# Attention and a residual MLP on one core: turning q and k in parts, other places for the weight sums, an earlier weight fetch and plain stores at the end

## The chip, the cores and the metric

The kernel runs on one core of a Trainium2 chip. The core has TensorE (PE, with its weight loads PEld), VectorE (DVE), ScalarE (ACT), GpSimd (POOL) and SyncE (SP), and 16 DMA engines that all of its queues share. The metric is the device time in microseconds of one execution; three runs of the kernel before gave 800.32, 802.85 and 801.59 us, a median of 801.59.

## The reference

Eight batches of 384 tokens. Grouped attention (16 query heads, 4 key heads, 64 wide) gives x of 384 x 1024 for each batch; then a token-mixing step and a two-layer MLP follow, each with a residual scaled by `lam`:

```python
scores = scale * np.matmul(q, k.transpose(0, 1, 3, 2))
attn = softmax(scores)
x = np.matmul(attn, v)                       # heads side by side: 384 x 1024
a1 = alpha1 * x + beta1
u = x + lam * np.einsum('ts,bsd->btd', w_tok, a1)
a2 = alpha2 * u + beta2
out = u + lam * (np.maximum(a2 @ w_ch1, 0.0) @ w_ch2)
```

`w_ch1` is 1024 x 4096, `w_ch2` 4096 x 1024. Inputs and output are float32.

## The kernel before

**Stages.** The attention of the first batch runs alone (`side(0)`). Then `main(0)` and `main(1)` compute the MLP of the first two batches, each in two phases: phase 0 is the first layer (32 row tiles of the hidden layer, bank `h`, L492), phase 1 the second (bank `ch`, L521). After that the six remaining batches go in three pairs, `pair(0)` to `pair(2)`; a pair does both of its layers with seven block products instead of eight, on sums and differences of blocks. Phase 0 of a pair is the first layer (banks X, Y, Z, L635), phase 1 the second (three banks C, one for each 128 tokens `ms`, L675), which runs through seven products `o` in the order 1, 2, 6, 5, 3, 7, 4 (`PLACE2`), each in two halves `h` of eight hidden tiles.

**Units and the plan.** Both generators `yield` after some matmuls; a yield is a unit. The order is written out by hand: `put(stage, phase, unit, work)` hangs work on a unit, and after that unit the work is emitted into the engines' queues, which run strictly in order. So the attention of the coming batches (`side(b)`) is strewn between the MLP's matmuls: `scores` (L272) and the exp on ACT (L281), `av` (L311, then on VectorE the chain L316, L319, L324, L326), `tok_flip` (L336, then L343, the spill of u to the output by SP at L236, L347, and the turn L359 by SP). In phase 1 of a pair a unit is four 512-wide matmuls; the side of the pair's first coming batch starts at unit 0, that of the second at unit 38.

**Turns.** q and k arrive by POOL's casting loads in `q_raw` and `k` and are turned to `qT` and `kT` by SP's transposing DMAs (`flip_q`, L168; `flip_k`, L164). There is one `qT` and one `kT`, so a turn waits for the scores that read them last. For a pair's second batch the five turns stood at units 33 to 37 of phase 1.

**Sums.** `sums_a(j)` (L534 to L537, four steps) forms the left operands from the turned tiles of both batches, so it waits for the turns L359. `sum_w1` (L571, L576) forms the sums of a group's two w1 chunks, `sum_w2` (L564) those of w2, which SP stores to DRAM (`w2s`, L551) and fetches back (L583) as 28 blocks for each pair.

**The ring.** w1 chunks and w2 blocks share six slots. When TensorE is done with a slot, `free` takes the next entry of `queue`: a casting load of a w1 chunk by POOL (L177) or a fetch of a w2 block by SP. Before, a next pair's first two chunks stood two entries ahead of the end of a pair's 28 fetches.

**Evictions and stores.** A product's result is read out of C by VectorE (L690, L695, L697), scaled by `lam` one unit or more later (`flush`, L606), and added into the output in DRAM by POOL's accumulating DMA (`store`, L477). In `main`, hidden tiles leave their bank by ACT (L500) or VectorE (L502), and the second layer's result by VectorE (L525).

Of the kernel before, what the change touches and what calls it, by code (L numbers as in the profile page):

```python
# [12 lines left out]
def kernel(  # L13
# [82 lines left out]
    def piece():  # L96
        i = turn[0] % 6
        turn[0] += 1
        return pad[:, i * 1024:(i + 1) * 1024]
# [60 lines left out]
        for h in range(0, Hq, G):  # L160
            nc.gpsimd.dma_start(out=qrs[b][:, h:h + G], in_=q[b, h:h + G].rearrange("h (p st) d -> p h st d", st=NST))

    def flip_k(b):
        nc.sync.dma_start_transpose(out=kT.rearrange("p h i s -> p (h i) s"),  # L164
                                    in_=k2s[b].rearrange("p h a st d -> p (h a st d)"))

    def flip_q(b, i=0, n=NP):
        nc.sync.dma_start_transpose(out=qT[:, i:i + n].rearrange("p a j s -> p (a j) s"),  # L168
# [312 lines left out]
    def main(b):  # L481
        a2T = a2Ts[b]
        n = S + 1 if b == 0 else S

        seq = order1[::-1 if b % 2 else 1]
        for i, c in enumerate(seq):
            for j in range(CW):
                nt = c * CW + j
                begun = b == 0 and nt in early
                ps = early[nt] if begun else bank([P, 512], "mm", "h")  # L490
                for dt in range(0 if begun else NDT):
                    nc.tensor.matmul(out=ps[:, :n], lhsT=w1[:, w1_slots[c], dt, j * P:(j + 1) * P],  # L492
                                     rhs=a2T[:, dt, :n], start=(dt == 0), stop=(dt == NDT - 1))
                    if dt == 3:
                        yield 0
                c1 = bias1[:, nt:nt + 1]
                if b == 0:
                    evac("DVE" if nt % 2 else "ACT")(out=c1, in_=ps[:, S:n])
                if nt % 2 == 0 or b:
                    nc.scalar.activation(out=hT[:, nt, :], in_=ps[:, :S], func=RELU, bias=c1)  # L500
                else:
                    nc.vector.tensor_scalar(out=hT[:, nt, :], in0=ps[:, :S], scalar1=c1,  # L502
                                            scalar2=0.0, op0=ADD, op1=mybir.AluOpType.max)
                yield 0
            if i + RING < NCH:
                w1_free.append(w1_slots.pop(c))
                load_w1(seq[i + RING])

            if b == 0 and i == NCH - RING:
                for dw, r, h in [(0, 1, 1)] + [(0, r, h) for r in (2, 3) for h in range(2)] + [  # L510
                        (1, r, h) for r in range(4) for h in range(2)]:
                    load_w2(dw, r, h)
                load_next(2)
        nts = [c * CW + j for c in seq for j in range(CW)]
        units = [(dw, ms) for dw in range(NDW) for ms in range(NST)]
        for k, (dw, ms) in enumerate(units):
            cs = slice(dw * 512, (dw + 1) * 512)
# [7 lines left out]
            nc.vector.tensor_tensor(out=o, in0=ps, in1=lam_t[:, cs], op=MUL)  # L525
# [59 lines left out]
    def free(slot):  # L585
        w1_free.append(slot)
        if queue:
# [1 line left out]
            f(*a)  # L589

    queue = [m for i in range(NB) for m in [(load_w1, c) for c in order1[2 if i else RING:]]
             + [(fetch, i, n) for n in range(SLOTS - 2)] + [(load_w1, c) for c in order1[:2] if i + 1 < NB]
             + [(fetch, i, n) for n in range(SLOTS - 2, SLOTS)]]

    IDENT = mybir.ActivationFunctionType.Identity
    SEQ1 = ((1, 0), (1, 1), (7, 0), (6, 0), (6, 1), (7, 1), (5, 0), (5, 1), (2, 0), (3, 0), (3, 1), (2, 1), (4, 0), (4, 1))
# [3 lines left out]
    def pair(i):  # L600
        b0 = NPL + 2 * i
        acc = pairs["acc"]

        def scaled(o, b, ms, dw, t):
            if o != 2:
# [61 lines left out]
        for k, o in enumerate(PLACE2):  # L667
            for h in range(2):
                for ms in range(NST):
                    if o == 4 and h and ms == NST - 1 and not last:  # L670
                        for n in (5, 7, 6, 4):
                            sum_w1(0, n)
                    for t in range(8 * h, 8 * h + 8):
                        slot = w2_slots[i, 4 * k + t // 4]
                        nc.tensor.matmul(out=X[ms], lhsT=hid[:, t, LEFT2[o], ms * P:(ms + 1) * P],  # L675
                                         rhs=ring[:, slot, t % 4 * 512:(t % 4 + 1) * 512],
                                         start=(o in (1, 6, 7) and t == 0), stop=(t == NH - 1), skip_group_check=True)
                        if t % 4 == 3 and ms == NST - 1:
                            free(slot)
                        if t % 8 == 3:  # L680
                            flush(1)
                            yield 1
                    if h == 1:
                        if o in (1, 6, 5):
                            q = ((1, 6, 5).index(o) * NST + ms) * 512
                            snap[o, ms] = snaps[:, q:q + 512]
                            if o == 1:
                                nc.scalar.copy(out=snap[o, ms], in_=X[ms])
                            else:
                                tt(out=snap[o, ms], in0=X[ms], in1=snap[1, ms], op=ADD)  # L690
                        else:
                            bb, dw = where[o]
                            t = spare(ms).bitcast(f32)
                            if o == 2:
                                tt(out=t, in0=X[ms], in1=lam_t[:, :512], op=MUL)  # L695
                            else:
                                tt(out=t, in0=X[ms], in1=snap[{3: 1, 7: 5, 4: 6}[o], ms], op=ADD)  # L697
                            later.append((scaled, o, b0 + bb, ms, dw, t))
                            if last and o == 4:
                                flush()  # L700
# [12 lines left out]
    with tc.manual_schedule(engines=order):  # L713
# [131 lines left out]
        def put(ps, phase, at, *m):  # L845
            plan.setdefault((ps, phase, at), []).append(m)
# [12 lines left out]
        put_all(0, 1, at)  # L859
        put_flips(0, 1, 2, (34, 36, 37, 42, 43))  # L860

        put(1, 0, 1, load_next, 3)
        put_all(1, 0, side(2)[1], lambda u: int(1.5 * u))
        put_flips(1, 0, 3, (53, 55, 57, 59, 61))
        put_all(1, 1, side(3)[1])
        for j, u in enumerate((33, 39, 43, 46)):
            put(1, 1, u, sums_a, j)
        for r in range(8):
            for i, o in enumerate((5, 6, 7, 4)):
                where = (1, 0, 30 + 16 * r + 4 * i) if r < 2 else (1, 1, 18 * (r - 2) + 4 * i) if r < 4 else (2, 0, 24 * (r - 4) + 1 + 6 * i)  # L870
# [61 lines left out]
```

## Time and profile before

| | before |
|---|---|
| runs, us | 800.32, 801.59, 802.85 |
| profiled execution, us | 794.35 |
| its span, first to last instruction, us | 792.5 |
| mean granted TensorE clock | 0.978 |
| TensorE busy, us | 745.1 |
| VectorE, ACT, POOL busy, us | 500.4, 327.3, 165.9 |
| from TensorE's last matmul to the end of the span, us | 8.1 |

TensorE and VectorE by stage (busy us of the length):

| stage | from to, us | TensorE | VectorE |
|---|---|---|---|
| `main(1)` phase 0 | 134 to 194 | 54.9 of 60 | 28.4 |
| `main(1)` phase 1 | 194 to 250 | 54.7 of 56 | 35.9 |
| `pair(0)` phase 0 | 250 to 332 | 77.5 of 82 | 65.7 |
| `pair(0)` phase 1 | 332 to 440 | 101.0 of 108 | 73.0 |
| `pair(1)` phase 0 | 440 to 524 | 77.0 of 84 | 59.2 |
| `pair(1)` phase 1 | 524 to 633 | 103.0 of 109 | 73.0 |
| `pair(2)` phase 0 | 633 to 712 | 74.5 of 79 | 58.6 |
| `pair(2)` phase 1 | 712 to 785 | 72.0 of 73 | 26.8 |

In the lines of a timeline the first number is the start in microseconds from the span's start, the second the duration; then come engine, source line, operation, the tiles (out<-in), the shape, and the count. Brackets hold the idle time of that engine just before, and what ended it. "SPq" is the DMA-issuing queue of SP; its duration is that of issuing, not of the transfer. In a list of waits the numbers are the total, how often, and the longest.

### The profile page before, as it was taken

What the parts mean: (1) busy time and instruction counts of PE and PEld (TensorE: products, weight loads), DVE (VectorE), ACT (ScalarE), POOL (GpSimd) and SP (SyncE); (2) the same over time, 40 slices, a digit from 0 to 9 for tenths busy, and PEclk for the clock granted to TensorE, in tenths of its full rate; (3) what the DMA queues carried; (4) which work ended last, traced back from release to release, by engine and by line L of the source; (5) the groups of instructions that cost most, each with busy time, mean ns of one, the idle gap of its engine ahead of it and who ended that gap; (6) DMA issues with size and microseconds to landing.
All of it is one profiled execution on the core that took longest, in us unless ns stands there. A gap on an engine that the chain in (4) does not pass through costs nothing.

```text
span 792.5 us, 14330 instructions
## 1 busy us (share of the span) xinstructions
PE 745.1 (94%) x5646; PEld 417.4 (53%) x5707; DVE 500.4 (63%) x975; ACT 327.3 (41%) x471; POOL 165.9 (21%) x214
## 2 busy tenths in 40 slices
PE   8999999998998999999997789999899889999995
PEld 5765555655554555555454356655445446654442
DVE  7663554454667788569576667738747677763333
ACT  7623332563340566643331266663233146660000
POOL 9434211410002310301022431121002221100012
PEclk9999999999998999999999899999999999999998
DMA  9999998999765999979889998997979999835786
GB/s 190 196 199 203 212 202 172 180 227 228 191 169 123 214 221 234 269 207 224 239 195 191 140 190 111 165 230 202 232 207 200 197 145 130 116 141 180 242 225 108
DMA packets 221536, 151.50 MB, mean 191 GB/s; under 512 B 92692, under 2 KB 200836, under 8 KB 221468
## 3 DMA queue, kind: packets, MB, share of 16 engines
q0 software_dynamic: 120736, 65.38, 63.4%
q1 hardware_dynamic: 100188, 84.80, 38.9%
q8 instruction: 44, 0.72, 0.4%
q10 hardware_dynamic: 544, 0.39, 0.2%
q14 instruction: 24, 0.20, 0.1%
HBM read 154.05 MB, written 38.27 MB: 243 GB/s over the span
## 4 chain that ended last, share of the span: by engine, by line
PE 68%; DMA 11%; issue 10%; DVE 7%; POOL 2%; ACT 1%; POOLq 0%; SPq 0%; DVEq 0%; ACTq 0%
PE C L675 15%; PE X L635 15%; PE ch L521 9%; PE Y L635 8%; DMA ops<-a 6%; PE h L492 6%; DMA w<-in_moe_w_ch_dram 4%; PE sc L272 4%; PE Z L635 4%; PE sc L336 2%; PE one L311 2%; PE sc L311 1%; POOL out_dram L477 1%; POOL w L177 1%; DMA qT<-q_raw 1%
## 5 line engine op out<-in xcount | busy, mean ns | idle before, releaser
L675 PE MATMUL C<-w,arena 128*128 128x512 bf16 x965 | 232.1, 383 | 2.4 <-issue 0.2
L281 ACT ACTIVATE es<-sc 128x1024 bf16<-128x1024 f32 x126 | 121.8, 1022 | 178.1 <-PE sc L272 171.8
L675 PEld LDWEIGHTS <-arena 128*128 128x128 bf16 x1008 | 92.8, 98 | 105.2 <-issue 11.1
L640 ACT ACTIVATE hT<-X,bias 128x384 f32<-128x384 f32 x144 | 83.7, 582 | 122.2 <-PE X L635 117.6
L635 PEld LDWEIGHTS <-w 128*128 128x128 bf16 x768 | 76.0, 99 | 70.9 <-issue 21.4
L477 POOL DMA_DIRECT2D out_dram<-hT x36 | 31.7, 881 | 283.0 <-DVE hT L606 179.8
L177 POOL DMA_DIRECT2D w<-in_moe_w_ch_dram x68 | 61.2, 906 | 141.7 <-PE X L635 63.2
L492 PE MATMUL h<-ops,w 128*128 128x384 bf16 (+1 forms) x480 | 84.4, 328 | 5.1 <-DMA w<-in_moe_w_ch_dram 3.6
L521 PE MATMUL ch<-arena,hT 128*128 128x512 bf16 x366 | 86.9, 379 | 0.9 <-issue 0.3
L635 PE MATMUL X<-ops,w 128*128 128x384 bf16 x384 | 72.7, 333 | 12.3 <-DVE hT L697 8.4
L635 PEld LDWEIGHTS <-pad 128*128 128x128 bf16 x576 | 57.5, 100 | 39.5 <-issue 3.7
L635 PE MATMUL X<-ops,pad 128*128 128x384 bf16 x384 | 73.3, 336 | 0.0
L492 PEld LDWEIGHTS <-w 128*128 128x128 bf16 x480 | 45.4, 98 | 35.5 <-DMA w<-in_moe_w_ch_dram 4.4
L343 DVE TENSOR_TENSOR xr<-sc,xr 128x384 f32<-128x384 f32 x56 | 31.1, 554 | 39.3 <-PE sc L336 39.3
L521 PEld LDWEIGHTS <-hT 128*128 128x128 bf16 x384 | 34.9, 98 | 37.7 <-issue 2.5
L336 PEld LDWEIGHTS <-wtokT 128*128 128x128 bf16 x576 | 37.7, 99 | 22.2 <-DVE a L326 12.7
L272 PE MATMUL sc<-qT,kT 64*128 64x384 bf16 (+2 forms) x576 | 44.7, 274 | 4.6 <-DMA qT<-q_raw 3.4
L311 PEld LDWEIGHTS <-es 128*128 128x128 bf16 x1008 | 39.4, 99 | 13.0 <-issue 1.2
L336 PE MATMUL sc<-a,wtokT 128*128 128x128 bf16 x504 | 38.3, 222 | 7.7 <-DVE a L326 7.6
L635 PE MATMUL Z<-ops,w 128*128 128x384 bf16 x192 | 39.0, 326 | 4.1 <-DVE arena L644 4.1
L635 PE MATMUL Y<-ops,w 128*128 128x384 bf16 x192 | 41.2, 339 | 0.3 <-DVE w L571 0.3
L642 DVE TENSOR_TENSOR arena<-Y,hT 128x384 bf16<-128x384 f32 x48 | 26.6, 557 | 23.1 <-ACT hT L640 20.9
(127 smaller groups left out, 835.8 us busy)
## 6 DMA issues: line engine op xcount, KB each, us to landing
w<-w2s SPq DMA_DIRECT2D x84, 512.0 KB, 5.0
w<-in_moe_w_ch_dram POOLq DMA_DIRECT2D x68, 512.0 KB, 9.3
out_dram<-xr SPq DMA_DIRECT2D x56, 192.0 KB, 4.7
out_dram<-hT POOLq DMA_DIRECT2D x36, 256.0 KB, 5.4
arena<-in_moe_w_ch_dram POOLq DMA_DIRECT2D x16, 512.0 KB, 19.1
w2s<-arena SPq DMA_DIRECT2D x28, 256.0 KB, 5.7
q_raw<-in_q_dram POOLq DMA_DIRECT2D x28, 192.0 KB, 8.9
w2s<-pad SPq DMA_DIRECT2D x16, 256.0 KB, 11.0
```

The source lines that it names most:

```text
L177: nc.gpsimd.dma_start(out=w1[:, w1_slots[c]], in_=w1src[:, :, c * CW * P:(c + 1) * CW * P])
L272: nc.tensor.matmul(out=sc[:, hh, k % 4:k % 4 + n], lhsT=kT[r, 2 * p // G, BLK[hh][sk], :], rhs=qT[r, p, st:st + n, :], start=True, stop=True)
L281: nc.scalar.activation(out=e, in_=sc, func=EXP, scale=scale_qk)
L311: nc.tensor.matmul(out=av[:, hh, sq, :], lhsT=ess[k // 4][:, m % 2, k % 4, :], rhs=vb[:, sk, hk, :], start=(sk == 0), stop=(sk == NST - 1))
L336: nc.tensor.matmul(out=ps[:, tt, :], lhsT=wtokT[:, st, tt * P:(tt + 1) * P], rhs=a1s[p][:, st, :], start=(st == 0), stop=(st == NST - 1 an ...
L343: nc.vector.tensor_tensor(out=u, in0=ps, in1=u, op=ADD)
L477: nc.gpsimd.dma_start(out=at, in_=o, accum_op=ADD)
L492: nc.tensor.matmul(out=ps[:, :n], lhsT=w1[:, w1_slots[c], dt, j * P:(j + 1) * P], rhs=a2T[:, dt, :n], start=(dt == 0), stop=(dt == NDT - 1))
L521: nc.tensor.matmul(out=ps, lhsT=hT[:, nt, ms * P:(ms + 1) * P], rhs=w2[:, row(nt)[0], row(nt)[1], cs], start=(i == 0), stop=(i == NNT - 1))
L635: nc.tensor.matmul(out=ps, lhsT=tb[g, o][:, dt, e * P:(e + 1) * P], rhs=opb(LEFT1[o])[:, dt], start=(o in (1, 2, 7) and dt == 0), stop=(dt ...
L640: nc.scalar.activation(out=snap[o, e], in_=ps, func=IDENT, bias=hi if o == 5 else lo)
L675: nc.tensor.matmul(out=X[ms], lhsT=hid[:, t, LEFT2[o], ms * P:(ms + 1) * P], rhs=ring[:, slot, t % 4 * 512:(t % 4 + 1) * 512], start=(o in ...
```

## The change

- `flip_k` takes a first head and a number of heads, and for a pair's second batch kT is turned in two parts and qT in four, at units 10, 17, 18, 25, 33 and 33 of phase 1. That batch's side starts at unit 36 instead of 38, and its `sums_a` stand at units 67, 71, 75, 79 (before 68, 72, 76, 80).
- In `main(1)`, odd hidden tiles are evicted by VectorE instead of ACT (16 of 32).
- In `queue`, a next pair's first two w1 chunks stand six fetches ahead of the end (before two).
- Their four sums `sum_w1(0, ...)` for the next pair stand at four places of the last product instead of together ahead of its last block.
- `load_next(3)` goes from unit 1 to unit 20 of `main(1)` phase 0; `sum_w2` keeps one row group there (before two) and has three in phase 1 (before two); `sums_a` and `sum_w1` of that stage have other units.
- In the last pair, the last product's part of the output is read back into SBUF during product 7, the product's other summand is scaled and added there (`begin_end`, `lift_end`), the last products are scaled and added on VectorE, and SP stores the result plainly. The last block is computed in three column parts of 256, 128 and 128.

```diff
-    def flip_k(b):
-        nc.sync.dma_start_transpose(out=kT.rearrange("p h i s -> p (h i) s"),
-                                    in_=k2s[b].rearrange("p h a st d -> p (h a st d)"))
+    def flip_k(b, h=0, n=Hkv):
+        nc.sync.dma_start_transpose(out=kT[:, h:h + n].rearrange("p h i s -> p (h i) s"),
+                                    in_=k2s[b][:, h:h + n].rearrange("p h a st d -> p (h a st d)"))
...
-                if nt % 2 == 0 or b:
+                if nt % 2 == 0:
                     nc.scalar.activation(out=hT[:, nt, :], in_=ps[:, :S], func=RELU, bias=c1)
...
-             + [(fetch, i, n) for n in range(SLOTS - 2)] + [(load_w1, c) for c in order1[:2] if i + 1 < NB]
-             + [(fetch, i, n) for n in range(SLOTS - 2, SLOTS)]]
+             + [(fetch, i, n) for n in range(SLOTS - 6)] + [(load_w1, c) for c in order1[:2] if i + 1 < NB]
+             + [(fetch, i, n) for n in range(SLOTS - 6, SLOTS)]]
...
+        ends = {}
+
+        def begin_end(ms):
+            ends[ms] = t = piece().bitcast(f32)
+            nc.sync.dma_start(out=t, in_=by_tok(out[b0 + 1])[:, ms, :512])
+
+        def lift_end(ms):
+            tt(out=snap[6, ms], in0=snap[6, ms], in1=lam_t[:, :512], op=MUL)
+            tt(out=ends[ms], in0=ends[ms], in1=snap[6, ms], op=ADD)
...
-                    if o == 4 and h and ms == NST - 1 and not last:
-                        for n in (5, 7, 6, 4):
-                            sum_w1(0, n)
-                    for t in range(8 * h, 8 * h + 8):
+                    if o == 4 and not last and (h, ms) in ((0, 1), (0, 2), (1, 0), (1, 1)):
+                        sum_w1(0, {(0, 1): 5, (0, 2): 7, (1, 0): 6, (1, 1): 4}[h, ms])
+                    if last and o == 7:
+                        (lift_end if h else begin_end)(ms)
+                    parts = ((0, 256), (256, 384), (384, 512)) if last and o == 4 and h and ms == NST - 1 else ((0, 512),)
+                    for (c0, c1), t in ((c, t) for c in parts for t in range(8 * h, 8 * h + 8)):
...
+                        if last and o == 4 and t == NH - 1:
+                            e, v = ends[ms][:, c0:c1], spare(ms).bitcast(f32)[:, c0:c1]
+                            tt(out=v, in0=X[ms][:, c0:c1], in1=lam_t[:, c0:c1], op=MUL)
+                            tt(out=e, in0=e, in1=v, op=ADD)
+                            nc.sync.dma_start(out=by_tok(out[b0 + 1])[:, ms, c0:c1], in_=e)
...
-        put(1, 0, 1, load_next, 3)
+        put(1, 0, 20, load_next, 3)
...
-        for j, u in enumerate((33, 39, 43, 46)):
+        for j, u in enumerate((38, 42, 45, 47)):
             put(1, 1, u, sums_a, j)
...
-                where = (1, 0, 30 + 16 * r + 4 * i) if r < 2 else (1, 1, 18 * (r - 2) + 4 * i) if r < 4 else (2, 0, 24 * (r - 4) + 1 + 6 * i)
+                where = (1, 0, 44 + 5 * i) if r < 1 else (1, 1, 12 * (r - 1) + 4 * i) if r < 4 else (2, 0, 24 * (r - 4) + 1 + 6 * i)
...
-            put(1, 1, 44 + i, sum_w1, 0, o)
+            put(1, 1, 38 + 2 * i, sum_w1, 0, o)
...
-            put_flips(ps, 1, c + 1, range(33, 38))
-            put_all(ps, 1, side(c + 1)[1], lambda u: u + 38)
+            for u, f, h in ((10, flip_q, 0), (17, flip_k, 0), (18, flip_q, 2), (25, flip_q, 4), (33, flip_k, 2), (33, flip_q, 6)):
+                put(ps, 1, u, f, c + 1, h, 2)
+            put_all(ps, 1, side(c + 1)[1], lambda u: u + 36)
             for j in range(4):
-                put(ps, 1, 38 + 4 * (j + 5) + 10, sums_a, j)
+                put(ps, 1, 36 + 4 * (j + 5) + 11, sums_a, j)
```

More of the change, by code (lines that the diff above doesn't have):

```diff
@@ L669, in pair @@
                 for ms in range(NST):
-                    if o == 4 and h and ms == NST - 1 and not last:
-                        for n in (5, 7, 6, 4):
-                            sum_w1(0, n)
-                    for t in range(8 * h, 8 * h + 8):
+                    if o == 4 and not last and (h, ms) in ((0, 1), (0, 2), (1, 0), (1, 1)):
[4 more added lines that the diff above has]
+                    for (c0, c1), t in ((c, t) for c in parts for t in range(8 * h, 8 * h + 8)):
                         slot = w2_slots[i, 4 * k + t // 4]
-                        nc.tensor.matmul(out=X[ms], lhsT=hid[:, t, LEFT2[o], ms * P:(ms + 1) * P],
-                                         rhs=ring[:, slot, t % 4 * 512:(t % 4 + 1) * 512],
+                        nc.tensor.matmul(out=X[ms][:, c0:c1], lhsT=hid[:, t, LEFT2[o], ms * P:(ms + 1) * P],
+                                         rhs=ring[:, slot, t % 4 * 512 + c0:t % 4 * 512 + c1],
                                          start=(o in (1, 6, 7) and t == 0), stop=(t == NH - 1), skip_group_check=True)
-                        if t % 4 == 3 and ms == NST - 1:
+                        if t % 4 == 3 and ms == NST - 1 and c1 == 512:
                             free(slot)
-                        if t % 8 == 3:
+                        if last and o == 4 and t == NH - 1:
[3 more added lines that the diff above has]
+                            nc.sync.dma_start(out=by_tok(out[b0 + 1])[:, ms, c0:c1], in_=e)
+                        if t % 8 == 3 and c1 == 512:
                             flush(1)
                             yield 1
-                    if h == 1:
+                    if h == 1 and not (last and o == 4):
                         if o in (1, 6, 5):
@@ L698, in pair @@
                             later.append((scaled, o, b0 + bb, ms, dw, t))
-                            if last and o == 4:
-                                flush()
                     if o in (2, 6) and (h, ms) in ((0, 1), (0, 2), (1, 0), (1, 1)):
```

## The prediction

> **What bounds the kernel now.** I read the shares of the engines first, then the list of waits, then TensorE's timeline for every idle stretch, and around each one the other engines.
>
> ```profile
> PE 745.1 (94%) x5646; PEld 417.4 (53%) x5707; DVE 500.4 (63%) x975; ACT 327.3 (41%) x471; POOL 165.9 (21%) x214
> ```
>
> TensorE is busy for 745.1 of 792.5 us, so 47.4 us of idle time, the slow clock behind long idle stretches, and the tail are all that an edit of order can win. The waits of TensorE (total, times, longest) say whom it waits for:
>
> ```profile
> PE X L635 <- DVE hT L697: 8.4, 2, 4.2
> PE sc L336 <- DVE a L326: 7.6, 5, 4.0
> PE Z L635 <- DVE arena L644: 4.1, 4, 2.8
> PE X L635 <- DVE o L525: 3.9, 1, 3.9
> PE h L492 <- DMA w<-in_moe_w_ch_dram: 3.6, 2, 2.2
> PE sc L272 <- DMA qT<-q_raw: 3.4, 2, 2.1
> ```
>
> The timelines (start, duration; in brackets the idle time before and its releaser) place them. First w1 chunks in the second batch's first layer, then the end of that batch:
>
> ```profile
> 180.51 1.32 PE L492 MATMUL h<-ops,w 128*128 128x384 bf16 x4 [2.22 <-DMA w<-in_moe_w_ch_dram]
> 191.02 1.47 PE L492 MATMUL h<-ops,w 128*128 128x384 bf16 x8 [1.41 <-DMA w<-in_moe_w_ch_dram]
> ...
> 252.50 0.68 DVE L525 TENSOR_TENSOR o<-ch,vecs 128x512 f32<-128x512 f32 x1
> 253.24 2.72 PE L635 MATMUL X<-ops,w 128*128 128x384 bf16 x8 [3.90 <-DVE o L525]
> ```
>
> Then the passage from one pair to the next. Twice VectorE stands still because a sum (L534) waits for a turned tile, with the eviction that frees TensorE's bank queued behind it:
>
> ```profile
> 414.56 3.11 SPq L359 DMA_TRANSPOSE ops<-a  x1
> 423.19 0.36 DVE L534 TENSOR_TENSOR ops<-ops 128x384 bf16<-128x384 bf16 x1 [3.57 <-DMA ops<-a]
> 427.14 1.14 PE L336 MATMUL sc<-a,wtokT 128*128 128x128 bf16 x9 [4.05 <-DVE a L326]
> 435.28 2.00 SPq L359 DMA_TRANSPOSE ops<-a  x1
> 442.78 0.36 DVE L534 TENSOR_TENSOR ops<-ops 128x384 bf16<-128x384 bf16 x1 [3.77 <-DMA ops<-a]
> 444.11 0.68 DVE L697 TENSOR_TENSOR hT<-C,hT 128x512 f32<-128x512 f32 x1
> 444.85 1.44 PE L635 MATMUL X<-ops,w 128*128 128x384 bf16 x4 [4.14 <-DVE hT L697]
> ```
>
> Last, a late w1 chunk in the second pair, scores waiting for the turn of q, and the tail:
>
> ```profile
> 472.41 0.69 DVE L576 TENSOR_TENSOR pad<-w 128x1024 bf16<-128x1024 bf16 x1 [3.83 <-DMA w<-in_moe_w_ch_dram]
> ...
> 572.92 3.96 SPq L168 DMA_TRANSPOSE qT<-q_raw  x3
> 573.58 1.04 PE L272 MATMUL sc<-qT,kT 64*128 64x384 bf16 x8 [2.05 <-DMA qT<-q_raw]
> ...
> 784.42 0.69 DVE L697 TENSOR_TENSOR hT<-C,hT 128x512 f32<-128x512 f32 x1 [0.31 <-PE C L675]
> 785.14 0.69 DVE L606 TENSOR_TENSOR hT<-hT,vecs 128x512 f32<-128x512 f32 x1
> 786.13 0.84 POOL L477 DMA_DIRECT2D out_dram<-hT  x1 [0.88 <-DVE hT L606]
> ```
>
> **The clock.** After the 2.05, 2.22 and 3.90 us stretches matmuls take twice as long for some microseconds; after 1.39 and 1.41 us they do not. The Trainium skill (TensorE: Matmul & The Clock Gate, "Why this matters for your kernels") asks only that idle gaps stay below about 3 us. The row at 573.58 contradicts it: eight score matmuls took 1.04 us after 2.05 us idle, against 0.61 after 1.39. By the page the 1.75 and 1.45 us of slow clock in parts 1 and 3 would not be there to win, and the sum would be 17.4 instead of 20.6.
>
> **Part 1, second batch's first layer (134 to 194 us): gain 5.8.** Three moves. `load_next(3)` goes from unit 1 to unit 20: its nine POOL issues now stand behind five w1 loads instead of ahead of all ten, and POOL no longer sits before them (it waited 13.6 us for the turn of k and 11.6 at the q loads, and issued the first three w1 loads together at 141.9). Of `sum_w2`, one row group (seven 256 KB stores) leaves this stage. The stalled chunks took about 20 us to land (160.2 to 180.5; 167.4 to 191.0), against a median of 9.3. Until the eighth chunk the new order has to move eight chunks of 0.52 MB, 1.34 MB of k, q, v and about 1.7 MB of spills and turns: 7.2 MB, at the stage's 209 GB/s 34 us, from 136 to 170, and it is needed at 178. Won: 2.22 + 1.41 idle, and slow clock at 180.5: (1.32-0.81)+(1.20-0.71)+(1.15-0.67)+(2.38-2.11) = 1.75. The 16 evictions that go from ACT (0.58 us each) to VectorE (618 ns in L502's row, 9.9 us in all) lie beside a VectorE that is busy 28.4 of 60 us; they remove 0.98 + 0.48 us behind exp on ACT, but queue behind the attention chain (0.20 + 3x0.59 = 2.0 us). Walking the eight places, three make TensorE wait 0.15 to 0.4 us: I take 1.0 against 1.46. Sum 5.4 + 0.5. Ends: -3 (all 16 evictions 0.4 late, half of the chunks' waits stay) and 7.
>
> **Part 2, from that batch to the first pair: 0.** VectorE is the bound from 239.9 us on. It had 2.0 us idle and the sums of w1 around the last eviction; now it has before it: one w2 sum 0.68, chain 2.0, four groups of `sums_a` less the last, 3x1.36, four w1 sums 2.74, two evictions 1.38, two pairs of L343/L347 2.3. That is 13.2 us and ends at 253.1; before it was 253.2. The idle stretch and its slow clock (24 matmuls in 6.8 us against 3.9) stay. Ends: -2 and +5.9 (idle down to 1).
>
> **Part 3, turns of q and k in parts: gain 5.5.** Six turns leave units 33 to 37 for places right after the scores that free each slice; kT becomes two turns of about half the 2.5 us issue. On SP they stand before fetches that have six blocks of lead, and cost them 1.25 us each: covered. What goes: 0.33+1.39 and 0.33+2.05 idle, slow clock (1.04-0.61)+(4.58-3.56, sixteen C matmuls in the chain of waits) = 1.45. VectorE's 8.0 us of idle time behind it also go. If VectorE's chain takes the place of the wait, 3.4; nothing supports more than 5.5.
>
> **Part 4, the passage between pairs, twice: gain 4.1.** I walk the queues from the fifth token matmul (time 0), with 0.862 us per unit of four C matmuls, 0.5 token, 0.55 AV, 0.52 scores. TensorE alone would reach the second X at 18.4. VectorE now has 326 of the last block done at 11.8 while TensorE wants it at 9.5: a 2.3 us wait by load alone, where the turn's 3.57 and 2.21 us stood before. The first three turns land well before their sums, five units later instead of four. Then `sums_a(1)`, a flush and the first w1 sum stand before L343 of the last block, so its turn is issued at 15.7; landing takes L; then `sums_a(3)` 1.36, a w1 sum 0.69, a flush 0.69, the eviction 0.69: second X at 19.2 + L. With 4.5 (median of L359) it is 5.2 us late, with 7.5 (both last turns before, beside two w1 loads) 8.2. The next w1 loads are still freed at unit 77, just beside the turn, so I take 7: 7.7 late. Before, by the same count, X was 10.4 and 9.1 late. Gain 2.7 + 1.4. Ends -1 (L 8.6, and TensorE's slow clock on top) and 9.1. The last six fetches now have four blocks of lead, 8.5 to 10.7 us, and three stand behind a spill and a turn on SP (up to 4.1 us); median landing 5.0, so covered by 0 to 1.6 us and by the stall itself.
>
> **Part 5, late chunk in the second pair: 2.3** of 2.84. After the restart the last pair's stores on POOL now wait only for a flush, no longer for four w1 sums (2.7 us); k, q, v and the w1 loads behind them move up by as much. Ends 0 and 2.8.
>
> **Part 6, the tail: 2.9.** From TensorE's end at 784.4 to 792.5 it is 8.1 us. The split block costs 8x109+16x56 ns = 1.77 against 1.73 (56 ns: nine 128-wide token matmuls in 0.5 us). VectorE's two steps at 128 columns are, extrapolated from 557 ns at 384 and 690 at 512, 0.29 each; with the backlog of the earlier parts it ends 1.2 after TensorE. SP's store landed in 2.4 (least) to 4.7 (median, L236); I take 4.0. Tail 5.2. The three reads and six VectorE steps for lifting lie under 5 us of C matmuls each. Ends 2.2 and 4.5. The Trainium skill (DMA: Bandwidth & Descriptors, "Issuing engines are not separate DMA queues") speaks against this part: another issuing queue saves only issue time. By it the landing would stay near 5.5 and the gain about 1.4; POOL's adding stores landed in 4.0 at least, SP's plain ones in 2.4.
>
> **Sum.** 5.8+0+5.5+4.1+2.3+2.9 = 20.6 us. The profiled execution took 794.35 us (span 792.5); it becomes 773.8. The median of the runs is 7.2 us above it; the same microseconds off 801.6 give **781.0**.
>
> **Rivals.** (a) Cleaner passage: turns land in 4.5, part 2 pays 5.9, tail 4.4: 5.8+5.9+5.5+9.1+2.8+4.4 = 33.5, time 768. For: the long landings stand beside w1 loads. Against: these stay beside the last turn. (b) VectorE takes over: parts 2 to 4 give nothing but 3.4: 5.8+3.4+2.3+2.9 = 14.4 and part 1 loses 3: 790. For: VectorE was continuously busy from 236.9 to 245.9. (c) Fetch lead: at the largest landing, 7.9, block 27 is 4.1+7.9-8.5 = 3.5 late and block 23 1.3, with slow clock 2.9: 7.7 for each of two pairs, time 796. For: it starts at a landing above 4.4; against: TensorE stands anyway. (d) Slower: score matmuls on other heads wait for a turned part, at three places of each pair's second layer. A part lands 3.4 (behind spill and turn) + 4.1 after its token matmul, the next scores stand 2.6 to 3.9 us on: waits of 4.9, 4.9, 3.6 and slow clock 3x1.45 make 17.8, twice 35.6: 817. It decides as soon as waits are kept for the whole of qT. Against: at 380.97 scores began when the first of four parts, issued at 377.85, had landed, while three were being issued until 383.8.
>
> **Chances.** Forecast (773 to 788) 0.52, (a) 0.15, (b) 0.15, (c) 0.10, (d) 0.05, anything else 0.03. What can be told from no change is 0.3%, 2.4 us. (a), (b), the forecast and most of (c) are faster by more: 0.88; same 0.05; slower 0.07. The range runs from (a) to between (b) and (c): 768 to 794; the forecast's own is 773 to 788.
>
> **What would show it.** No wait of L492 on w1 loads over 1 us near 180 and 191; no wait of L272 on qT; TensorE still waiting 3 to 6 us on the eviction at each passage (L697 before) and some 4 us on L525 at about 245; a tail of about 5 us. A wait of C matmuls on w2s fetches shows (c); scores waiting on qT after units 10 to 25 show (d); a landing of the last turn of 4.5 us would make part 4 wrong upward.

## The result and the profile after

Four runs of the changed kernel gave 787.39 to 790.47 us, median 789.07; four of the kernel before beside them 800.32 to 803.29, median 802.22. The ratio is 0.984 (95% interval 0.981 to 0.987): 13.2 us faster. It is inside the whole range of the prediction (768 to 794) and on the side that was forecast, but above the forecast's own 773 to 788; the forecast for the median was 781.0, a gain of 20.6. The profiled execution took 787.39 us (span 785.5, mean granted clock 0.983) against 794.35 before, so the two profiles differ by 7.0 us only.

First the engines' line of the page, then the list of TensorE's waits (total, times, longest):

```profile
PE 740.0 (94%) x5662; PEld 415.5 (53%) x5723; DVE 512.1 (65%) x1001; ACT 318.9 (41%) x455; POOL 163.4 (21%) x211
```

```profile
PE X L645 <- DVE hT L714: 11.8, 2, 7.3
PE Z L645 <- DVE arena L654: 5.2, 4, 3.9
PE C L687 <- DMA w<-w2s: 4.6, 3, 2.4
PE h L492 <- DMA w<-in_moe_w_ch_dram: 3.8, 3, 1.6
PE X L645 <- DVE o L525: 3.3, 1, 3.3
PE sc L336 <- DVE a L326: 2.5, 2, 1.4
```

Against the list of before: the scores' wait on qT (3.4) is gone and that of the token matmuls L336 is down from 7.6 to 2.5, but the restart of X in the next pair waits 11.8 us instead of 8.4, and a wait that was not there before has come, C on fetched w2 blocks (4.6).

To see where time went, the program is cut at its own marks: the starts of the first L521 matmul of each `main`, of the first and the last L645 matmul of a pair (L635 before), and of the last C matmul. The lengths of these stretches in the profiled executions (two of before and two of the change; the second ones, and u_queue and best1, are from the experiments below), in us:

| stretch | before | the change | u_queue | best1 |
|---|---|---|---|---|
| `main(0)` phase 1 with `main(1)` phase 0 | 117.8, 119.5 | 117.1, 118.0 | 116.9 | 117.5 |
| `main(1)` phase 1 | 59.1, 59.6 | 58.5, 58.5 | 58.4 | 58.3 |
| `pair(0)` phase 0 | 77.4, 76.1 | 75.9, 79.2 | 76.9 | 77.4 |
| `pair(0)` phase 1 | 109.3, 110.0 | 104.9, 106.7 | 106.8 | 105.2 |
| `pair(1)` phase 0, with the restart's wait | 82.7, 85.0 | 85.2, 86.0 | 81.3 | 80.9 |
| `pair(1)` phase 1 | 110.0, 109.0 | 105.9, 107.2 | 104.2 | 104.3 |
| `pair(2)` phase 0, with the restart's wait | 79.0, 78.8 | 82.6, 80.9 | 79.6 | 73.5 |
| `pair(2)` phase 1 | 72.5, 72.5 | 76.5, 76.7 | 76.6 | 74.3 |
| last C matmul to the end | 8.5, 8.6 | 3.6, 3.6 | 3.6 | 3.6 |

The third row is the same code in every kernel here and lies between 75.9 and 79.8 in thirteen profiled executions: that much a single execution scatters in one stretch. Most of this is one wait of TensorE for the bank Z, whose eviction stands on VectorE behind the sum of a late w1 chunk: it is 2.4 to 3.7 us in the five longest of these thirteen (3.00 in the second execution of the change, at 281.8 us) and absent in others. The table shows the story of the change: the second layers lose 2 to 4 us each, the following first layers take 1 to 4 us back, and the last layer gives up 4 of the 5 us that the end gains.

The w1 chunks of part 1, in TensorE's timeline, and the DMA view of that stage (134 to 192 us):

```profile
172.82 2.12 PE L492 MATMUL h<-ops,w 128*128 128x384 bf16 x12 [1.56 <-DMA w<-in_moe_w_ch_dram]
184.44 2.12 PE L492 MATMUL h<-ops,w 128*128 128x384 bf16 x12 [0.63 <-DMA w<-in_moe_w_ch_dram]
189.29 1.47 PE L492 MATMUL h<-ops,w 128*128 128x384 bf16 x8 [1.57 <-DMA w<-in_moe_w_ch_dram]
```

```profile
DMA packets 24399, 11.04 MB, mean 190 GB/s; under 512 B 10570, under 2 KB 23882, under 8 KB 24394
...
q0 software_dynamic: 15152, 6.62, 94.7%
```

The chunks are as late as before in sum (3.8 against 3.6 us). The stage moves 11.0 instead of 12.5 MB, but at 190 GB/s instead of 209, and the time that the packets of POOL's queue (q0) took is now 95% of the DMA engines' time there (before 82%; the shares of the queues overlap and add up to more than 100).

The passage from `pair(1)` to `pair(2)`, the timeline of several engines:

```profile
603.40 1.02 PE L687 MATMUL C<-w,arena 128*128 128x512 bf16 x3 [2.44 <-DMA w<-w2s]
613.88 0.68 PE L336 MATMUL sc<-a,wtokT 128*128 128x128 bf16 x9 [1.15 <-DVE a L326]
616.62 2.11 POOL L177 DMA_DIRECT2D w<-in_moe_w_ch_dram  x2
617.50 2.24 SPq L359 DMA_TRANSPOSE ops<-a  x1
627.58 0.36 DVE L534 TENSOR_TENSOR ops<-ops 128x384 bf16<-128x384 bf16 x1 [7.04 <-DMA ops<-a]
630.12 0.68 DVE L714 TENSOR_TENSOR hT<-C,hT 128x512 f32<-128x512 f32 x1
630.85 1.44 PE L645 MATMUL X<-ops,w 128*128 128x384 bf16 x4 [7.33 <-DVE hT L714]
```

After the end of the last token matmuls 2.9 us pass until the last turn is issued, 0.9 us behind two w1 loads; it lands 10.1 us later, VectorE stands for it with the eviction behind it, and X restarts 3.3 us after the landing. Before, this wait was 4.2.

The end, in the timeline:

```profile
757.85 1.44 SPq L608 DMA_DIRECT2D pad<-out_dram  x3
766.87 0.69 DVE L612 TENSOR_TENSOR pad<-pad,hT 128x512 f32<-128x512 f32 x1 [7.37 <-DMA pad<-out_dram]
770.75 1.89 PE L687 MATMUL C<-w,arena 128*128 128x512 bf16 x7 [0.64 <-DVE hT L714]
773.27 2.97 PE L687 MATMUL C<-w,arena 128*128 128x512 bf16 x13 [0.64 <-DVE hT L714]
780.45 0.61 PE L687 MATMUL C<-w,arena 128*128 128x128 bf16 x8 [0.97 <-DVE hT L694]
781.44 0.61 PE L687 MATMUL C<-w,arena 128*128 128x128 bf16 x8 [0.38 <-DVE hT L694]
```

The first read of the output lands after 9 us; VectorE stands 7.4 us for it, with evictions behind it, and TensorE waits for these. At the column parts TensorE waits until VectorE has read the part before out of the same bank.

### The profile page after: what moved, and what is told of

Its sections match the earlier page's. It is cut to its first block, busy times and chain, and to the rows that moved or that the text cites. A ratio compares the mean times of both kernels' runs of the same rounds, so it can differ in the third digit from the quotient of the medians.

```text
span 785.5 us, 14382 instructions
## 1 busy us (share of the span) xinstructions
PE 740.0 (94%) x5662; PEld 415.5 (53%) x5723; DVE 512.1 (65%) x1001; ACT 318.9 (41%) x455; POOL 163.4 (21%) x211
## 4 chain that ended last, share of the span: by engine, by line
PE 65%; DMA 15%; issue 9%; DVE 7%; POOL 2%; ACT 1%; SPq 1%; POOLq 0%; DVEq 0%; ACTq 0%
PE C L687 18%; PE X L645 14%; PE Y L645 7%; PE ch L521 6%; PE h L492 6%; DMA w<-in_moe_w_ch_dram 5%; DMA ops<-a 4%; PE Z L645 3%; PE sc L272 3%; DMA arena<-in_moe_w_ch_dram 3%; PE sc L336 2%; DMA w<-w2s 2%; PE one L311 1%; DMA pad<-out_dram 1%; PE sc L311 1%
## 5 line engine op out<-in xcount | busy, mean ns | idle before, releaser
L687 PE MATMUL C<-w,arena 128*128 128x512 bf16 (+2 forms) x981 | 230.3, 376 | 9.9 <-DMA w<-w2s 4.6
L650 ACT ACTIVATE hT<-X,bias 128x384 f32<-128x384 f32 x144 | 83.9, 583 | 123.1 <-PE X L645 118.7
L645 PEld LDWEIGHTS <-w 128*128 128x128 bf16 x768 | 76.4, 100 | 74.6 <-issue 26.8
L521 PE MATMUL ch<-arena,hT 128*128 128x512 bf16 x366 | 87.1, 379 | 1.6 <-DMA arena<-in_moe_w_ch_dram 0.6
L645 PE MATMUL X<-ops,w 128*128 128x384 bf16 x384 | 73.7, 336 | 15.1 <-DVE hT L714 11.8
L645 PEld LDWEIGHTS <-pad 128*128 128x128 bf16 x576 | 57.4, 100 | 39.5 <-issue 3.6
L645 PE MATMUL X<-ops,pad 128*128 128x384 bf16 x384 | 72.5, 333 | 0.0
L521 PEld LDWEIGHTS <-hT 128*128 128x128 bf16 x384 | 34.9, 98 | 38.5 <-issue 3.4
L343 DVE TENSOR_TENSOR xr<-sc,xr 128x384 f32<-128x384 f32 x56 | 31.0, 554 | 34.8 <-PE sc L336 34.8
L336 PEld LDWEIGHTS <-wtokT 128*128 128x128 bf16 x576 | 37.2, 98 | 16.2 <-DVE a L326 6.1
L645 PE MATMUL Z<-ops,w 128*128 128x384 bf16 x192 | 39.0, 326 | 5.2 <-DVE arena L654 5.2
L645 PE MATMUL Y<-ops,w 128*128 128x384 bf16 x192 | 40.5, 335 | 0.0
L336 PE MATMUL sc<-a,wtokT 128*128 128x128 bf16 x504 | 37.3, 219 | 2.6 <-DVE a L326 2.5
```

Of the source, the lines that this page charges most:

```text
L336: nc.tensor.matmul(out=ps[:, tt, :], lhsT=wtokT[:, st, tt * P:(tt + 1) * P], rhs=a1s[p][:, st, :], start=(st == 0), stop=(st == NST - 1 an ...
L343: nc.vector.tensor_tensor(out=u, in0=ps, in1=u, op=ADD)
L645: nc.tensor.matmul(out=ps, lhsT=tb[g, o][:, dt, e * P:(e + 1) * P], rhs=opb(LEFT1[o])[:, dt], start=(o in (1, 2, 7) and dt == 0), stop=(dt ...
L650: nc.scalar.activation(out=snap[o, e], in_=ps, func=IDENT, bias=hi if o == 5 else lo)
L687: nc.tensor.matmul(out=X[ms][:, c0:c1], lhsT=hid[:, t, LEFT2[o], ms * P:(ms + 1) * P], rhs=ring[:, slot, t % 4 * 512 + c0:t % 4 * 512 + c1 ...
```

## The experiments

Twelve kernels ran in three sets of four, each set on one chip with its own runs of the kernel before (medians 800.42, 798.87 and 798.18 us). Times are compared inside a set, and ratios are to its runs of before.

**First set: one part of the change undone at a time.**

u_turns undoes the turns in parts and the earlier side (with the old units of its `sums_a`):

```diff
-            for u, f, h in ((10, flip_q, 0), (17, flip_k, 0), (18, flip_q, 2), (25, flip_q, 4), (33, flip_k, 2), (33, flip_q, 6)):
-                put(ps, 1, u, f, c + 1, h, 2)
-            put_all(ps, 1, side(c + 1)[1], lambda u: u + 36)
+            put_flips(ps, 1, c + 1, range(33, 38))
+            put_all(ps, 1, side(c + 1)[1], lambda u: u + 38)
```

> The changed kernel with one part undone: for a pair's second batch q and k are turned at units 33 to 37 again, the side starts at unit 38 and its sums stand at 68 to 80. Theory (the turns are worth what the trace of before shows, 1.7 and 3.8 us of waits and slow clock in pairs 0 and 1, and nothing replaces them): 4.5 to 6.5 us slower than the changed kernel's 789.1, so 793.5 to 795.5, and the waits of L272 on qT return. Rival (VectorE's chain takes the place of the wait, so the turns were worth little): at most 2.5 us slower, under 791.6.

Measured 792.11 us, ratio 0.988 [0.985, 0.991]. The waits for qT are back:

```profile
383.17 0.61 PE L272 MATMUL sc<-qT,kT 64*128 64x384 bf16 x8 [2.61 <-DMA qT<-q_raw]
574.67 0.76 PE L272 MATMUL sc<-qT,kT 64*128 64x384 bf16 x8 [1.90 <-DMA qT<-q_raw]
```

Beside u_tail, the nearest to the change in this set (789.65; the change itself did not run in it), the median is 2.5 us slower, of the 5.5 forecast. But the intervals of the two ratios (u_tail 0.985 to 0.990) lie on each other, and from the last L645 matmul of `pair(0)` to that of `pair(2)` the profiled execution of u_turns took 378.9 us, as much as the change (379.0 in the mean of five). So the waits that the turns in parts remove are shown; that the whole kernel gains by them, with the queue and the sums as the change has them, is not. The time lies between the two expectations.

u_main undoes `main(1)`'s edits and the evictions by VectorE:

```diff
-                if nt % 2 == 0:
+                if nt % 2 == 0 or b:
...
-        put(1, 0, 20, load_next, 3)
+        put(1, 0, 1, load_next, 3)
```

(and the old units of `sums_a`, `sum_w2` and `sum_w1` of that stage).

> The changed kernel with the second batch's MLP as before: load_next(3) at unit 1, two row groups of w2 sums in the first layer, the old units of the sums, and all of its hidden tiles evicted by ACT. Theory (from the trace after: TensorE still waits 3.8 us for w1 chunks there, so only the slow clock and 0.5 us went): 1.5 to 3.5 us slower than 789.1, 790.6 to 792.6. Rival (the prediction's part 1, chunks early and all waits gone): 5 to 7 us slower, 794 to 796.

Measured 793.58 us (788.73 to 799.22, twelve runs), ratio 0.991 [0.988, 0.994], again between the two. The stretches say more than the total: the first two rows of the table are 118.7 + 59.4 us here, and the same in the mean of the three executions with the old code (this one and the two of before), against 117.5 + 58.4 in the mean of the ten with the new one. Up to there the part is worth 2.1 us. The stretch after it, the third row, gives some of it back: 76.8 us in the mean of the three and 77.9 in that of the ten, where Z's wait of the third row (0.7 us or more) came in seven, and in none of the three. Whether the new code brings that wait about stays open.

u_queue puts the fetch queue and the four w1 sums back:

```diff
-             + [(fetch, i, n) for n in range(SLOTS - 6)] + [(load_w1, c) for c in order1[:2] if i + 1 < NB]
+             + [(fetch, i, n) for n in range(SLOTS - 2)] + [(load_w1, c) for c in order1[:2] if i + 1 < NB]
...
-                    if o == 4 and not last and (h, ms) in ((0, 1), (0, 2), (1, 0), (1, 1)):
-                        sum_w1(0, {(0, 1): 5, (0, 2): 7, (1, 0): 6, (1, 1): 4}[h, ms])
+                    if o == 4 and h and ms == NST - 1 and not last:
+                        for n in (5, 7, 6, 4):
+                            sum_w1(0, n)
```

> The changed kernel with a next pair's first two w1 chunks two fetches ahead of the end again, and its four w1 sums together ahead of the last block again. Theory (the earlier chunks took the waits for turned tiles of 3.6 and 2.2 us away and brought waits for w2s blocks of 4.6 us in all, an exchange): within 2.5 us of 789.1, and no wait of C matmuls on w2s fetches, while the first sum of each passage waits for its turn again. Rival (parts 4 and 5 of the prediction, 6.4 us): 4 us or more slower, over 793.

Measured 781.42 us (778.48 to 783.21), ratio 0.977 [0.974, 0.980]. Both expectations missed: these two edits of the change cost time, 8.2 us beside u_tail, or 7.7 without the 0.5 of the end, which u_tail lacks (see below). The passage from `pair(1)` to `pair(2)`:

```profile
613.05 2.12 POOL L177 DMA_DIRECT2D w<-in_moe_w_ch_dram  x2
613.33 2.23 SPq L359 DMA_TRANSPOSE ops<-a  x1
622.00 0.36 DVE L534 TENSOR_TENSOR ops<-ops 128x384 bf16<-128x384 bf16 x1 [4.75 <-DMA ops<-a]
624.67 1.44 PE L645 MATMUL X<-ops,w 128*128 128x384 bf16 x4 [4.05 <-DVE hT L715]
```

The turn still stands behind two w1 loads, but lands in 8.7 us, and X restarts 2.7 us after it, because no w1 sum stands before the eviction. C's wait of 2.44 on block 23 is gone; waits for block 27 (1.98 and 1.04) stay, although the queue is the old one again. Both passages together are 7.5 us shorter than with the change (108.8 against 112.6 each, from the last L645 matmul of a pair to the restart of X in the next): the passages account for what the two edits cost.

u_tail has the old end (no reads, no column parts, POOL's adding stores):

> The changed kernel with the end as before: no reading back of the output, whole last block, results added in DRAM by POOL. Theory (tail 8.1 again instead of 3.4, but 1.7 us of waits behind the lifting steps and 1.35 us between the column parts go): 1 to 2.5 us slower than 789.1, 790 to 791.6. Rival (prediction's part 6, nothing paid for it in TensorE's time): 2.9 us or more slower, 792 and over.

Measured 789.65 us, ratio 0.988 [0.985, 0.990], just below the theory's range; the rival's 792 and over did not come. Its last pair's phase 1 is 72.5 us long and the end 8.8, as before. Together that is 81.3 us, and 81.1 in the mean of the three executions with the old end, against 80.6 in the mean of the six that have the change's end (80.2 to 81.0). The end is worth 0.5 us.

**Second set: the two edits of u_queue apart, the late read, and a better version.**

q_only puts only the queue back, s_only only the w1 sums (the two halves of the diff of u_queue).

> Only the order of the fetch queue goes back: the next w1 chunks stand two blocks before the end of the w2 fetches instead of six; the four sums of w1 stay spread over the last block. The version with both undone ran in 781.4 against 789.1. Theory Q (the short lead of the last six fetches is the cost, because C waits 2.44 and 1.77 us on w2s there and the two w1 loads that are then in flight lie beside the last turn): 781 to 783, no wait of C on w2s over 1.2 us at block 23, and a restart of X less than 5 us late after both pairs. Theory S (the sums of w1, 0.69 us each, stand ahead of the eviction on VectorE): 787 to 790, restarts stay 4.5 and 7 us late. If both pay half each: 784 to 786.

> Only the four sums of w1 go back together, ahead of the last eight token units of the pair's last block; the fetch queue stays as the change has it. Theory Q: 787 to 790, with the waits of C on w2s of 2.4 and 1.8 us still there and the restarts of X 4 to 7 us late. Theory S: 781 to 783, the waits on w2s still there but the restarts of X at most 2 and 4 us late. Both half each: 784 to 786.

Measured 786.65 us for q_only (ratio 0.986 [0.981, 0.990]) and 787.86 for s_only (0.987 [0.983, 0.991]). The profiled execution of s_only was 8 us above its median and is left out. Beside m_read of this set (790.34, the change with the reads moved) their medians are 3.7 and 2.5 us lower, together 6.2. Their intervals overlap with that of m_read (0.985 to 0.993) and with each other, so the runs show what the two edits cost together (u_queue), and not which of them costs how much. In q_only's profile no C matmul waits for block 23 any more and the restarts are 2.7 and 4.6 us late, as theory Q expected of the trace, but not of the time; waits of 2.6 and 1.5 us for block 27 remain.

m_read issues the three reads two products earlier:

```diff
-                    if last and o == 7:
-                        (lift_end if h else begin_end)(ms)
+                    if last and o == 5 and not h:
+                        begin_end(ms)
+                    if last and o == 7 and h:
+                        lift_end(ms)
```

> The change with the three reads of the output for the tail issued two products earlier (the product left of 5 instead of that of 7), some 14 us. Theory (the end gained little because VectorE stood 7.4 us for a read that landed after 9 us, so that its evictions held up TensorE three times, 0.41 + 0.64 + 0.64): 1.7 us less than the change, 787.0 to 788.0, and no wait of VectorE at L612. Rival (those three waits are filled again by TensorE's waits further on, on the last block's eviction): within 0.6 of the change, 788.5 to 789.7.

Measured 790.34 us, ratio 0.989 [0.985, 0.993], which by itself says nothing for the theory. The stretch does: the last pair's phase 1 is 74.34 us against 76.5 and 76.7, and VectorE does not wait at L612:

```profile
742.68 1.44 SPq L608 DMA_DIRECT2D pad<-out_dram  x3
...
771.26 0.69 DVE L612 TENSOR_TENSOR pad<-pad,hT 128x512 f32<-128x512 f32 x1
```

So the late read costs 2.2 us where it stands, and the total hides it in the scatter of the other stretches.

best1 is u_queue with one of the four steps, `sums_a(1)`, later (unit 74 instead of 71; the others keep 67, 75 and 79) and the reads early:

```diff
-                put(ps, 1, 36 + 4 * (j + 5) + 11, sums_a, j)
+                put(ps, 1, (67, 74, 75, 79)[j], sums_a, j)
```

> The version with fetch queue and w1 sums undone (781.4), and with it the four groups of sums_a placed at units 67, 74, 75 and 79 of the second layer, that is the last ones after the eviction that the next pair waits for, and the reads for the tail two products earlier. Theory (VectorE's queue ahead of the eviction sets the restart, and the late read the tail): restarts of X from 1.07 and 4.05 us late to 0 and 2, so 2 to 3 us, and 1.5 us at the end: 777 to 779. Rival (the last turn's landing sets the restart whatever stands on VectorE, and the tail is filled again): 780.5 to 782.

Measured 775.15 us (773.18 to 778.45), ratio 0.971 [0.967, 0.975]: better than both kernels. The expected 777 to 779 us, laid against the first set's 800.42, are 0.971 to 0.973, so it is at the lower end of what the theory said. The same passage in its timeline:

```profile
614.22 1.32 SPq L359 DMA_TRANSPOSE ops<-a  x1
614.98 1.82 POOL L177 DMA_DIRECT2D w<-in_moe_w_ch_dram  x2 [1.01 <-PE C L690]
619.77 0.36 DVE L534 TENSOR_TENSOR ops<-ops 128x384 bf16<-128x384 bf16 x1 [0.46 <-DMA ops<-a]
621.87 1.46 PE L645 MATMUL X<-ops,w 128*128 128x384 bf16 x8
```

With `sums_a(1)` no longer ahead of L343 the turn is issued 1.3 us after the end of the last token matmuls (change 2.9, u_queue 2.3), and 0.8 us ahead of the two w1 loads. It lands in 5.6 us, and X does not wait. At the other passage it lands in 7.5 us and X waits 0.75.

**Third set: both kernels once more, and two versions further.**

> The kernel before once more, for a second profiled execution of it: the first took 794.35 us, the runs beside it 800.3 to 803.3, so the sum of the prediction was made against an execution some 8 us shorter than the others. Theory (the runs differ by how long the late w1 chunks and the restarts stall TensorE and what clock follows): an execution of 799 to 803 us shows the restarts of X over 5 us late or the w1 waits of L492 over 5 us in sum, and stages of the first layers some us longer. Rival (the clock alone, everywhere): waits as in the first, and every stage longer by the same 1 per cent.

Measured 799.28 us (796.16 to 805.57, twelve runs), ratio to the set's other runs of before 1.003 [1.000, 1.005]. The profiled execution was again one of the shortest (796.16), its waits like those of the first. What makes other executions of this kernel take 800 to 805 us stands in no profile here. But each run has its mean granted clock on record, and in this set's 35 runs of before the two go together: 0.982 to 0.986 in the three shortest (794.5 to 795.3 us), 0.974 in the four longest (803.9 to 805.6). Where in the kernel the clock was lower stays open.

> The changed kernel once more, on the chip of the three beside it. Theory: ratio to before 0.984 as in the first comparison, the second layers of the pairs some 4 us shorter than before, the restarts of X 4.5 to 7.3 us late, the last pair's second layer 4 us longer than before and the end 5 us shorter. Rival (the first comparison was a lucky one): ratio 0.989 or more, as u_turns, u_main and the version with early reads had.

Measured 794.14 us (787.96 to 798.76, twelve runs), ratio 0.994 [0.991, 0.997]: 4.0 us faster than before on this chip, not 13. The stretches are much as the theory expected (restarts 5.4 and 5.3 us late, last phase 1 76.7, end 3.6, the pairs' second layers 2 to 3 us shorter instead of 4), the ratio is the rival's. So the size of the first comparison, four runs against four, does not hold on another chip; that the change is faster does.

best2 is best1 with the second batch's side at unit 37, and best3 is best2 with the last block whole:

```diff
-            put_all(ps, 1, side(c + 1)[1], lambda u: u + 36)
+            put_all(ps, 1, side(c + 1)[1], lambda u: u + 37)
...
-                    parts = ((0, 256), (256, 384), (384, 512)) if last and o == 4 and h and ms == NST - 1 else ((0, 512),)
+                    parts = ((0, 512),)
```

> The 775.15 us version (fetch queue and w1 sums undone, last sums_a late, early reads) with the side of a pair's second batch one unit later (37 instead of 36), so that the fetch of block 27 is issued before the spill and the turn that stood ahead of it on SP. Theory: the waits of C on w2s (2.10 and 1.14 us) go, 2 to 4 us less, ratio 0.966 to 0.969. Rival (the turns, a unit later, make the restarts of X late again): X 1 to 3 us late and the ratio 0.970 to 0.974.

> As the one beside it, but the last product of the last block whole, not in column parts of 256, 128 and 128. Theory (the parts cost what they gain, since TensorE waits for VectorE's read of the earlier columns): the last pair's second layer 1 to 2 us shorter, the stretch from TensorE's end to the end as much longer, the same time within 1 us. Rival (the parts are what shortens the end): the second layer 0.5 us shorter and the end 2 to 3 us longer, 2 us slower.

best2: 781.72 us, ratio 0.982 [0.978, 0.985], worse than the expectation of either side. No C matmul waits for w2s any more, but the turn is again issued 0.6 us behind the two w1 loads, lands in 7.0 and 7.2 us, and the restarts are late:

```profile
PE X L645 <- DVE hT L717: 7.9, 2, 4.1
```

best3: 783.37 us, ratio 0.981 [0.977, 0.984], against best2 the same, as the theory expected. Its last phase 1 is 72.5 us (best2 74.3) and its end 5.2 (3.6): the column parts cost 1.9 and gain 1.6.

## Why the prediction was right in direction and too large in size

By stretches, in means over the profiled executions with the code in question (old code for the first line: before, before_2, u_main; passages of the change for the second: after, after_2, u_main, u_tail, m_read; old end for the third: before, before_2, u_tail; the change's end: after, after_2, u_turns, u_main, u_queue, q_only):

| parts | forecast | measured | how |
|---|---|---|---|
| 1 and 2 | 5.8 + 0 | 2.1 | 178.0 to 175.9, first two rows |
| 3, 4 and 5 | 5.5 + 4.1 + 2.3 | 2.9 | 381.9 to 379.0, both passages and both first layers after them |
| 6 | 2.9 | 0.5 | 81.1 to 80.6, last phase 1 and end |
| sum | 20.6 | 5.5 | |

`pair(0)` phase 0 is not in this sum; with the 1.0 us that it takes back, 4.5 are left. The two comparisons gave 13.2 and 4.0. The sum by stretches agrees with the second. The first is 8.7 above it; no stretch shows where that would be, and it stays open. That the first comparison's 789.07 us lie near rival (b)'s 790 is luck: (b) has VectorE as the bound of the passages, but there VectorE stood idle for the turn (7.0 us at 627.58).

**Part 1** failed at its step "7.2 MB, at the stage's 209 GB/s 34 us, from 136 to 170, and it is needed at 178". The rate was taken as fixed and every transfer as equal. In fact it fell to 190 GB/s with POOL's queue at 95% of the engines' time, k, q and v now between the fifth and the sixth w1 load, and the last five loads landed in 12.3 to 21.6 us. In the first profile of the change no wait was over 1.6 us and no slow clock followed; in the other nine executions with this code one of 1.9 to 2.9 us came all the same. The waits behind exp on ACT fell from 1.5 to 1.0 us, as said. The first row of the table gained 1.2 us of the 5.8.

**Part 2**, nothing, was a little low: the second row lost 1.0 us in the mean. X still waited on L525, 3.3 us instead of 3.9.

**Part 3** was right in mechanism: no wait on qT is left, and nothing like rival (d) is in the trace, so turned parts are released one by one. The trace gain up to the restart is 2.6 us at each passage beside u_turns (last L645 to restart: 112.6, mean of ten, against 115.1, mean of two), as forecast. It did not last: u_turns' first layers after the restarts were as much shorter, and its median of 2.5 us more is not clear of the scatter.

**Part 4** is where the sum broke. From the last L645 matmul to the restart a passage took 114.6 us before (four) and 112.6 with the change (ten): 2.0 for parts 3 and 4 together, where 4.8 were forecast. Two terms were off. "So I take 7" for the last turn's landing: it was 9.3 in the mean of ten (8.3 to 10.2; before 7.5), above even the 8.6 of the lower end. And the six blocks' lead, "covered by 0 to 1.6 us and by the stall itself": block 23 came 2.44 late, block 27 1.77. That is the mechanism of rival (c); it was priced at 7.7 a pair and given 0.10. Only block 23 belongs to the lead: block 27 is waited for with the old queue too (u_queue, q_only, best1), and no longer in best2, where the side starts a unit later. u_queue, with both edits back, takes 108.8 for a passage and q_only 109.6, so the 4.8 were there to be had from the turns in parts and the earlier side; the queue and the w1 sums ahead of the eviction gave them back. Why the turn lands so late was not isolated: issued ahead of the two w1 loads (best1) it took 5.6 and 7.5 us, behind them 6.6 to 7.8 (before, best2, best3) and 8.3 to 10.2 (the change).

**Part 5** did not come: Z waits 3.9 us at 467.87 (before 2.84; 4.6 in before_2). The first step came: k's load is issued 3.2 us after the restart instead of 5.6. But it lands 16.3 us after it instead of 15.7 (before_2 16.3), and the w1 load whose sum stands ahead of Z's eviction is issued at 18.8 and lands at 28.0 (before 18.4 and 27.5, before_2 18.9 and 28.1). So the stores that VectorE had held up were not what set it. Two w1 loads now fall into the first 14 us after the restart (landed at 9.5 and 13.9), where before one did (13.4) and the other had landed at 2.7.

**Part 6** had its gain too small and its price missing. The end lost 4.9 us, not 2.9: SP's last store of 64 KB landed in 1.5 us, where 4.0 was taken. But "the three reads and six VectorE steps for lifting lie under 5 us of C matmuls each" left out the landing of the read, 9.1 us beside the fetches, with evictions queued behind it on VectorE (2.2 us, m_read), and TensorE's wait for VectorE between the column parts (1.9 us, best3). The Trainium skill (DMA: Bandwidth & Descriptors, "Issuing engines are not separate DMA queues") would have only the issue time saved at the end, 1.4 in the prediction. best3, with whole stores of 256 KB as before, ends 3.3 us sooner after its last matmul than the kernel before, so here more than that was saved; whether by the queue or by not adding in DRAM no run tells apart.

**The base.** The sum was laid against a profiled execution 7.2 us below the median. The second profile of before was low as well, so a median cannot be reached from these stretches to better than some us.

## What to carry to other kernels

Where an eviction stands in line behind a sum that waits for a DMA, look at what that DMA is issued behind: a turn issued 1.1 us sooner and ahead of two weight loads took that wait from 4.1 us (u_queue) to none (best1) in one profile of each, and all that had moved at that place was one `sums_a` step, from ahead of L343 to behind L347. Price an added read or an earlier fetch by its landing in that place and by who stands behind the one that waits for it, not by engine steps. And where executions scatter by 1%, compare stretches between the program's own marks: they showed 2 us effects that totals of five rounds hid.

## What the runs showed of the hardware

**Idle time and clock.** Over thirteen profiled executions, after their first 100 us: of 63 idle stretches of TensorE between 0.9 and 1.9 us none was followed, among the next ten matmuls, by one that took over 1.3 times the usual for its kind; of 32 between 1.9 and 3.0 us 17 were, of 29 between 3.0 and 4.1 us 21, of 23 longer ones 22. The prediction's reading (slow after 2.05, not after 1.41) and the Trainium skill's bound of about 3 us (TensorE: Matmul & The Clock Gate, "Why this matters for your kernels") are both too sharp: in q_only twenty C matmuls after 2.63 us idle took 4.48 us, in u_queue the same twenty after 1.98 us took 6.16. The prediction's own row at 573.58 has a twin: in before_2 the same eight score matmuls took 0.61 us after 2.04 us idle, not 1.04. What decides between 1.9 and 4 us was not found.

**Landing of a transposing DMA.** The same 128-token turn landed in 5.6 to 10.2 us, depending on what was issued around it.

**A bank in parts.** A matmul into columns 256 to 383 of a bank waited until VectorE had read columns 0 to 255 (0.97 and 0.38 us for the two later parts), although the columns differ. Whether the chip or the program's own ordering asks for this no run tells.
